# Mixing an attention output inside the attention's own tile shapes, in plain float32, with a new set of planner costs

## The chip, the cores and the metric

The kernel runs on 1 core of one Trainium2 chip. TensorE (PE) does the matmuls, and its weight loads are listed apart as PEld. VectorE (DVE), ScalarE (ACT), GpSimd (POOL) and SyncE (SP) each run their own instructions in the order in which they were written down; they wait for each other only through semaphores. The metric is the device time of the core in microseconds (us).

## The reference

```
scores = (1/sqrt(64)) * q @ k.T                  # 4 batches x 12 heads, 448 x 448
scores = cap * tanh(scores / cap)
attn   = softmax(scores)                         # rows of 448
x      = attn @ v, heads side by side            # 4 x 448 x 768
h      = x.T @ U @ V                             # U 448 x 32, V 32 x 448: mixes the 448 tokens
u      = x + h.T
out    = u + relu(u @ w_ch1) @ w_ch2             # 768 -> 3072 -> 768
```

## The kernel before, in words

The kernel keeps `u` transposed: for each batch one tile `u0` to `u3` of 128 partitions (two heads of 64) by 6 head pairs by 448 tokens. There are 24 head pairs in all.

The **attention stage** is written in groups of four head pairs (`four`). A score tile holds the two heads of a pair, each in 64 rows of the array (`scores`, line 459); ACT then does `tanh` on it (464), and one `exp` for two tiles (474). The products with `v` are lines 488 (the last 64 keys, 64x64 tiles) and 500 (128x64 tiles). DVE adds the exponentials up (506), and for every two pairs PE sums them over the partitions in 128x32 tiles (`sums`, 539 and 542). The sums are copied to `sr`, go through two small DMAs and a reciprocal on DVE, come back broadcast as `rb` (563), and DVE multiplies `u` by them (568).

The **mixing** (`mixin`, 12 times, each for two head pairs) is what is changed. Per mixing, PE turns `u` round in two steps of four transposes (590), ACT or DVE copies each result to `xx` as float32r (`high`), DVE subtracts that from the original to keep the lost low bits (`low`, 601), PE multiplies high and low parts with `ust`, which holds U in four blocks, the last of them U's own low bits (606, 4 matmuls of 256 columns in each step), the result `yp` is copied to `ys` and a low part of it made (617), and two matmuls with `vst` (626) give the two tiles `hh` that DVE adds to `u` (630). All these matmuls are float32r or transposes in the full 128x128 shape of the array; scores, products with `v` and sums are plain float32 in smaller tiles that run side by side.

The **second stage** (MoE in the code's names) is `u @ w_ch1`, relu and `@ w_ch2` in float32r matmuls of 448 columns (829, 894, 1021), on high and low parts, with Strassen-like savings. DVE and ACT make their operands. Some results are poured onto `u` by a DMA from a tile `st` (907).

The **order** on every engine is made when the kernel is built. Each piece is a task with a cost for each engine that may do it, a priority and its buffers; `simulate` runs the tasks through a list scheduler: when an engine is free it starts the ready task of the lowest priority number for which there are buffers. A task on PE whose `mode` differs from that of the task ahead is charged `SWITCH` (210) more. The tag `misc` has two PSUM banks, shared by sums, transposes, `yp` and `hh`. `fill` puts 18 dummy matmuls (385) into the first 25 us.

Of the kernel before, what the change touches and what calls it, by code (L numbers as in the profile page):

```python
# [11 lines left out]
F32 = mybir.dt.float32  # L12
F32R = mybir.dt.float32r
# [3 lines left out]
ALU = mybir.AluOpType  # L17

B, H, S, D = 4, 12, 448, 64
DM = H * D  # L20
FF = 4 * DM
R = 32
# [3 lines left out]
KT = 4  # L26
TM = S // KT
# [55 lines left out]

LAT = {"PE": 240, "ACT": 110, "DVE": 110, "POOL": 150, "SP": 0}
SWITCH = 210


class Plan:
# [43 lines left out]
    def simulate(self):  # L132
# [3 lines left out]
        mode = dict.fromkeys(LAT)  # L136
        head = dict.fromkeys(self.order, 0)
        locked = {"DVE": 0, "POOL": 0}
        events, out, now = [], [], 0
# [1 line left out]
            if not t.wait:  # L141
                heapq.heappush(events, (t.begin, 0, t.i, "r"))

        def room(b):
            if self.order[b.tag][head[b.tag]] is not b:
                return None
            for p in b.pools:
                if p.free[p.at(b)] and all(not q.due for q in p.after):
                    return p
            return None  # L150

        def can(t, e):
            if any(b.pool is None and not room(b) for b in t.bufs):
                return False
            if t.lock and e in locked and locked["POOL" if e == "DVE" else "DVE"] > now:
                return False
            if len(t.durs) > 1:
                for o, d in t.durs.items():
                    if o != e and d < t.durs[e]:
                        queue = sum(x.durs[o] for x in ready[o] if x is not t and (x.prio, x.i) < (t.prio, t.i))  # L160
                        if max(free[o] - now, 0) + queue + d <= t.durs[e]:
                            return False
            return True

        def start(t, e):
            for b in t.bufs:
                if b.pool is None:
                    p = room(b)
                    p.free[p.at(b)] -= 1
                    b.pool = p  # L170
                    b.slot = p.idle[p.at(b)].pop(0)
                    head[b.tag] += 1
            cost = t.durs[e] + (SWITCH if t.mode != mode[e] else 0)
            mode[e] = t.mode
            t.at, t.eng = now, e
            out.append(t)
            free[e] = now + cost
            if t.lock and e in locked:
                locked[e] = now + cost
            for o in t.durs:  # L180
                ready[o].remove(t)
            heapq.heappush(events, (now + cost, 1, t.i, "e"))
            heapq.heappush(events, (now + cost + (LAT[e] if t.lat is None else t.lat), 2, t.i, "d"))

        while True:
            for e in LAT:
# [7 lines left out]
            now = events[0][0]  # L194
            while events and events[0][0] == now:
                _, _, i, what = heapq.heappop(events)
                t = self.tasks[i]
# [63 lines left out]
class Build(Plan):  # L261
# [75 lines left out]
    def mixing_consts(self):  # L337
        nc = self.nc
        begin, prio = 15000, -150
        raw = self.buf("wr", [128, 2 * DM], I32, self.wq)  # L340
        raw2 = self.buf("wr", [128, 2 * DM], I32, self.wq)
        a, a2 = (self.buf("wa", [128, DM], F32, self.wp) for _ in range(2))
        n = KT * R
        ust = self.ust = self.buf("ust", [TM, KT, 4, R], F32R, self.aq)
        vst = self.vst = self.buf("vst", [128, S], F32R, self.aq)

        def load():
            nc.sync.dma_start(out=self.ident, in_=self.id_dram)
            nc.sync.dma_start(out=raw.t[:TM, :2 * n], in_=self.u.bitcast(I32))

        def load2():
            nc.sync.dma_start(out=raw2.t[:, :2 * S], in_=self.vv.bitcast(I32))

        def u_parts():
            ur = a.t[:TM, :n].rearrange("p (t r) -> p t r", t=KT)
            for i in range(3):
                nc.vector.tensor_copy(ust.t[:, :, i], ur)
            nc.vector.tensor_tensor(out=ust.t[:, :, 3], in0=ur, in1=ust.t[:, :, 0].bitcast(F32), op=ALU.subtract)

        def v_parts():  # L360
            vr = a2.t[:, :S]
            nc.vector.tensor_copy(vst.t, vr)
            nc.vector.tensor_tensor(
                out=vst.t[64:96], in0=vr[64:96], in1=vst.t[64:96].bitcast(F32), op=ALU.subtract)

        self.task({"SP": 700}, load, w=[(raw, "u"), (raw, "l"), ("ident", 0)], lat=4000, begin=begin, prio=prio)
        self.task({"SP": 400}, load2, w=[(raw2, "u"), (raw2, "l")], lat=4500, begin=begin, prio=prio)
        self.convert(raw, lambda: raw.t[:TM, :2 * n], a, lambda: a.t[:TM, :n], prio, n)
        self.task({"DVE": 800}, u_parts, r=[(a, 0)], w=[(ust, 0)], prio=prio)
        self.convert(raw2, lambda: raw2.t[:, :2 * S], a2, lambda: a2.t[:, :S], prio, S)  # L370
        self.task({"DVE": 900}, v_parts, r=[(a2, 0)], w=[(vst, 0)], prio=prio)


    def fill(self):
# [42 lines left out]
    def four(self, p):  # L417


        nc = self.nc  # L420
# [3 lines left out]
        for i in range(4):  # L424
            b, q = divmod(p + i, NP)
# [18 lines left out]
        for g in range(7):  # L444
# [3 lines left out]
            for j in range(2):  # L448
# [16 lines left out]

                r = [(qks[c], 0) for c in cs]
                if j == 0:
                    self.task({"PE": 750}, scores, r=r, w=[(ps, 0), (pss[1], "next")], prio=prio, mode="q" if t == 3 else "sc")
                else:
                    self.task({"PE": 750}, scores, r=[*r, (pss[1], "next")], w=[(ps, 0)], prio=-300, mode="q" if t == 3 else "sc")  # L470
                self.task({"ACT": 920}, tanh, r=[(ps, 0)], w=[(th, j)], prio=prio)
# [101 lines left out]
    def mixin(self, b, pp):  # L573

        nc = self.nc
        p = b * NP + 2 * pp + 1
        prio = p - 100
        u = self.u_bufs[b]
        yp = None
        ks = [(u, 2 * pp), (u, 2 * pp + 1)]  # L580
        for t0 in (0, 2):
            tp = self.psum("misc")
            yp = yp or self.psum("misc")
            xx = self.buf("xx", [TM, 2, 2, 256], F32R, self.aq)

            def transposes(t0=t0, tp=tp):
                for j in range(2):
                    for i in range(2):
                        tok = TM * (t0 + j)
                        nc.tensor.transpose(  # L590
                            tp.t[:TM, 256 * j + 128 * i:256 * j + 128 * i + 128], u.t[:, 2 * pp + i, tok:tok + TM],
                            self.ident)

            def view(tp):
                return tp.t[:TM].rearrange("p (t n) -> p t n", t=2)

            def high(e, tp=tp, xx=xx):
                self.copy(e, xx.t[:, 0], view(tp))

            def low(tp=tp, xx=xx):  # L600
                nc.vector.tensor_tensor(out=xx.t[:, 1], in0=view(tp), in1=xx.t[:, 0].bitcast(F32), op=ALU.subtract)

            def products(t0=t0, xx=xx):
                for i in range(2):
                    for j in range(2):
                        nc.tensor.matmul(
                            yp.t[:, :256], self.ust.t[:, t0 + j], xx.t[:, i, j], start=t0 + j + i == 0,
                            stop=t0 + j == KT - 1 and i == 1)

            self.task({"PE": 450}, transposes, r=[*ks, ("ident", 0)], w=[(tp, 0)], prio=prio, mode="mm")  # L610
            self.task({"ACT": 600, "DVE": 690}, high, r=[(tp, 0)], w=[(xx, 0)], prio=prio)
            self.task({"DVE": 690}, low, r=[(tp, 0), (xx, 0)], w=[(xx, 1)], prio=prio)
            self.task({"PE": 480}, products, r=[(xx, 0), (xx, 1), (self.ust, 0)], w=[(yp, 0)], prio=prio, mode="mm")
        ys = self.buf("ys", [128, 256], F32R, self.an)

        def y_low():
            nc.vector.tensor_tensor(
                out=ys.t[32:64], in0=yp.t[32:64, :256], in1=ys.t[32:64].bitcast(F32), op=ALU.subtract)

        self.task({"ACT": 380, "DVE": 400}, lambda e: self.copy(e, ys.t, yp.t[:, :256]), r=[(yp, 0)], w=[(ys, 0)], prio=prio)  # L620
        self.task({"DVE": 420}, y_low, r=[(yp, 0)], w=[(ys, 0)], prio=prio)
        for i in range(2):
            hh = self.psum("misc")

            def mix(i=i, hh=hh):
                nc.tensor.matmul(hh.t[:, :S], ys.t[:, 128 * i:128 * i + 128], self.vst.t, start=True, stop=True)

            def add(i=i, hh=hh):
                x = u.t[:, 2 * pp + i]
                nc.vector.tensor_tensor(out=x, in0=x, in1=hh.t[:, :S], op=ALU.add)  # L630

            self.task({"PE": 210}, mix, r=[(ys, 0), (self.vst, 0)], w=[(hh, 0)], prio=prio, mode="mm")
            self.task({"DVE": 620}, add, r=[(hh, 0)], w=[ks[i]], prio=prio)


# [472 lines left out]
```

## Time and profile before

| | |
|---|---|
| median of 3 runs | 866.02 us (864.76 to 869.65) |
| profiled execution, first to last instruction | 867.9 us |
| PE busy | 851.3 us (98%) |
| DVE busy | 678.5 us (78%) |
| ACT busy | 518.2 us (60%) |
| mean granted clock | 0.996 |

Of the profiled execution the span is the only time listed; it lies 1.9 us above the median and inside the range of the runs. Matmuls are pipelined, and PE counts as busy while one is under way, so 98% doesn't say that PE is at its peak: time that PE loses between two matmuls of different shapes is inside it. Where one group of matmuls starts and where the next one starts says more than the busy column.

### The profile page before, as it was taken

The numbers are of one execution on the slowest core, as the hardware profiler recorded it, in microseconds if no ns is written. First come the engines' busy times: TensorE is split into PE (matmuls) and PEld (weight loads), VectorE is DVE, ScalarE is ACT, GpSimd is POOL, SyncE is SP. The second block draws the span as 40 slices with busy tenths as digits, with TensorE's granted clock in tenths as the row PEclk, the third lists the DMA queues.
The fourth block names the chain that finished last, engine by engine and source line by source line (L and its number), as shares of the span: only waits on it lengthen the run. The fifth ranks groups of instructions, "written<-read, shape, count | busy, mean of one in ns | idle before, by whom it ended". The sixth has DMA issues, their size and how long they took to land.

```text
span 867.9 us, 11802 instructions
## 1 busy us (share of the span) xinstructions
PE 851.3 (98%) x4314; PEld 677.4 (78%) x4314; DVE 678.5 (78%) x1131; ACT 518.2 (60%) x771; POOL 134.2 (15%) x174
## 2 busy tenths in 40 slices
PE   9999998999999999998999999999999999999998
PEld 5343442435899999997999999999999999999997
DVE  2798887867987777876777789788888788888864
ACT  7999897987554555535554455455655555555610
POOL 0111111111121111211111111101111111211110
PEclk9999999999999999999999999999999999999999
DMA  6753344422578787897887754914426354452413
GB/s 220 251 166 102 119 140 133 129 65 60 147 212 263 207 248 204 221 244 215 220 249 203 231 161 92 269 40 98 133 43 163 77 137 96 78 164 42 98 33 128
DMA packets 49338, 132.38 MB, mean 153 GB/s; under 512 B 6496, under 2 KB 25344, under 8 KB 49280
## 3 DMA queue, kind: packets, MB, share of 16 engines
q1 hardware_dynamic: 23024, 79.29, 28.3%
q0 software_dynamic: 19344, 33.46, 21.3%
q10 hardware_dynamic: 6912, 18.88, 5.5%
q8 instruction: 34, 0.56, 0.3%
q14 instruction: 24, 0.20, 0.1%
HBM read 79.28 MB, written 24.47 MB: 120 GB/s over the span
## 4 chain that ended last, share of the span: by engine, by line
PE 53%; DVE 0%; issue 0%
PE mm L829 25%; PE mm L1021 15%; PE mm L894 13%; DVE cx L842 0%; DVE u L899 0%; DVE wa L308 0%
## 5 line engine op out<-in xcount | busy, mean ns | idle before, releaser
L829 PE MATMUL mm<-x,ws 128*128 128x448 f32 x1512 | 333.6, 367 | 1.2 <-DVE x L664 1.2
L829 PEld LDWEIGHTS mm<-x,ws 128*128 128x128 f32 x1512 | 283.7, 188 | 27.4 <-DVE x L664 1.5
L894 PE MATMUL mm<-g,w 128*128 128x448 f32 x864 | 188.1, 367 | 2.5 <-ACT st L254 2.0
L894 PEld LDWEIGHTS mm<-g,w 128*128 128x128 f32 x864 | 162.8, 189 | 17.3 <-ACT st L254 2.4
L1021 PE MATMUL mm<-g,w 128*128 128x448 f32 x630 | 139.9, 366 | 0.0
L254 ACT ACTIVATE st<-mm 128x448 f32<-128x448 f32 x121 | 65.9, 545 | 120.1 <-PE mm L894 61.8
L1021 PEld LDWEIGHTS mm<-g,w 128*128 128x128 f32 x630 | 118.2, 188 | 10.6
L907 POOL DMA_DIRECT2D u<-st x72 | 62.9, 873 | 265.1 <-ACT st L254 265.1
L464 ACT ACTIVATE th<-sc,qsc 128x896 f32<-128x896 f32 x84 | 80.5, 1005 | 11.2 <-PE sc L459 7.0
L899 DVE TENSOR_TENSOR u<-u,mm 128x448 f32<-128x448 f32 x96 | 59.4, 620 | 34.1 <-PE mm L894 32.3
L459 PE MATMUL sc<-qk 64*128 64x448 f32 (+1 forms) x384 | 76.8, 567 | 1.2 <-ACT th L464 1.2
L474 ACT ACTIVATE th<-th,capt 128x1792 f32<-128x1792 f32 x42 | 75.3, 1794 | 1.0
L1044 POOL DMA_DIRECT2D u<-st x45 | 38.8, 863 | 218.8 <-ACT st L254 173.8
L500 PE MATMUL o<-th,vn 128*64 128x448 f32 x288 | 59.4, 548 | 0.0
L664 DVE TENSOR_TENSOR ws<-ta,ws 128x384 fp32r<-128x384 f32 x96 | 52.9, 552 | 7.0 <-ACT ws L254 6.6
L308 DVE SCALAR_TENSOR_TENSOR wa<-wa,wr 128x768 int32<-128x768 int32 (+2 forms) x50 | 46.7, 936 | 14.1 <-ACT wa L300 13.2
L459 PEld LDWEIGHTS sc<-qk 64*128 64x128 f32 (+1 forms) x384 | 26.8, 173 | 34.4 <-issue 18.8
L506 DVE TENSOR_TENSOR es<-es,th 128x896 f32<-128x896 f32 (+1 forms) x36 | 39.1, 1087 | 11.6 <-ACT th L474 11.1
L300 ACT ACTIVATE wa<-wr 128x768 f32<-128x768 f32 (+2 forms) x50 | 44.0, 884 | 3.9 <-DMA kept<-wa 1.8
L254 ACT ACTIVATE cx<-mm 128x448 f32<-128x448 f32 x42 | 22.9, 545 | 38.0 <-PE mm L829 24.6
L500 PEld LDWEIGHTS o<-th,vn 128*64 128x64 f32 x288 | 18.5, 136 | 34.5 <-issue 32.4
L1039 DVE TENSOR_TENSOR u<-u,mm 128x448 f32<-128x448 f32 x45 | 27.9, 620 | 22.3 <-PE mm L1021 20.9
(116 smaller groups left out, 984.4 us busy)
## 6 DMA issues: line engine op xcount, KB each, us to landing
wr<-in_w SPq DMA_DIRECT2D x48, 768.0 KB, 5.8
u<-st POOLq DMA_DIRECT2D x117, 224.0 KB, 4.1
kept<-wa ACTq DMA_DIRECT2D x48, 384.0 KB, 5.9
qk<-in_qk SPq DMA_DIRECT2D x24, 448.0 KB, 4.1
wa<-kept SPq DMA_DIRECT2D x28, 384.0 KB, 4.0
wr<-kept SPq DMA_DIRECT2D x20, 384.0 KB, 4.0
vn<-in_v SPq DMA_DIRECT2D x12, 448.0 KB, 3.9
rb<-rd POOLq DMA_DIRECT2D x24, 224.0 KB, 3.9
```

Of the source, the lines that this page charges most:

```text
L254: e.activation(out=out, in_=in_, func=func)
L308: nc.vector.scalar_tensor_tensor(out=a_t().bitcast(I32), in0=a_t().bitcast(I32), scalar=3, in1=raw_t()[:, 0::2], op0=ALU.logical_shift_lef ...
L459: nc.tensor.matmul(ps.t[out, a, :S], qks[c].t[hd, 1, 128 * t:min(S, 128 * t + 128)], qks[c].t[hd, 0], start=True, stop=True)
L464: nc.scalar.activation(out=th.t[:, j], in_=ps.t[:, :, :S], func=AF.Tanh, scale=self.qsc)
L474: nc.scalar.activation(out=th.t, in_=th.t, func=AF.Exp, scale=self.capt)
L500: nc.tensor.matmul(o.t[64 * a:64 * a + 64, :S], vn.t[:, 3 * i + t, a], th.t[:, j, a], start=False, stop=t == 2)
L664: e.tensor_tensor(out=lo, in0=src(), in1=hi.bitcast(F32), op=ALU.subtract)
L829: nc.tensor.matmul(ps.t[:, :S], ws[p].t[:, wi, sl], xs[p].t[:, xi, d], start=fresh and n == 0, stop=n == 8, skip_group_check=not fresh)
L894: nc.tensor.matmul(ps.t[:, :S], w1[f].t[:, wi, sl], g[b, f].t[:, gi], start=f == fs[0] and i == 0, stop=f == fs[-1] and i == 2)
L899: nc.vector.tensor_tensor(out=u.t[:, d], in0=u.t[:, d], in1=ps.t[:, :S], op=ALU.add)
L907: nc.gpsimd.dma_start(out=u.t[:, d], in_=st.t, accum_op=ALU.add)
L1021: nc.tensor.matmul(ps.t[:, :S], w[:, wi, k, sl], g[gi][:, k], start=fresh and n == 0, stop=n == 5, skip_group_check=not fresh)
```

## The change

**The mixing.** One step of 16 transposes takes the place of two steps of four: each turns one head's 64 rows by 112 tokens, the two heads of a pair go into two `misc` banks, and their task has the mode `sc` of the score tiles. Two copies (ACT or DVE) put them into one float32 `xx`; no low parts are made. The products with U are 8 plain float32 matmuls of 128 columns into 32 partitions each (mode `s`, that of the sums), `ys` is 128 columns wide rather than 256, and the products with V are two plain float32 matmuls in 64 rows each (mode `sc`). `ust` holds U once, `vst` V, both float32.

**The planner.** ACT and DVE tasks occupy their engine for 75 and 60 less than their cost (`OVER`), and their results still come at the full cost. A task can now take several buffers of one tag at once (`rooms`). The first score tile of each two gets a priority lower by 3. As the order of all engines comes out of one simulation, it changes in the second stage too.

```diff
+OVER = {"ACT": 75, "DVE": 60}
...
-            cost = t.durs[e] + (SWITCH if t.mode != mode[e] else 0)
+            new = [b for b in t.bufs if b.pool is None]
+            for b, p in zip(new, rooms(new)):
...
+            cost = max(t.durs[e] - OVER.get(e, 0), 60) + (SWITCH if t.mode != mode[e] else 0)
...
-            heapq.heappush(events, (now + cost + (LAT[e] if t.lat is None else t.lat), 2, t.i, "d"))
+            heapq.heappush(events, (now + cost + OVER.get(e, 0) + (LAT[e] if t.lat is None else t.lat), 2, t.i, "d"))
...
-                    self.task({"PE": 750}, scores, r=r, w=[(ps, 0), (pss[1], "next")], prio=prio, mode="q" if t == 3 else "sc")
+                    self.task({"PE": 750}, scores, r=r, w=[(ps, 0), (pss[1], "next")], prio=prio - 3, mode="q" if t == 3 else "sc")
...
-            def low(tp=tp, xx=xx):
-                nc.vector.tensor_tensor(out=xx.t[:, 1], in0=view(tp), in1=xx.t[:, 0].bitcast(F32), op=ALU.subtract)
...
+        tps = [self.psum("misc") for _ in range(2)]
+        xx = self.buf("xx", [TM, KT, 2, 128], F32, self.aq)
+
+        def transposes():
+            for i in range(2):
+                for t in range(KT):
+                    for a in range(2):
+                        hd = slice(64 * a, 64 * a + 64)
+                        at = 64 * (2 * t + i)
                         nc.tensor.transpose(
+                            tps[a].t[:TM, at:at + 64], u.t[hd, 2 * pp + i, TM * t:TM * t + TM], self.ident[hd, hd])
+
+        self.task({"PE": 480}, transposes, r=[*ks, ("ident", 0)], w=[(tp, 0) for tp in tps], prio=prio, mode="sc")
+        for a, tp in enumerate(tps):
+            self.task({"ACT": 520, "DVE": 640}, lambda e, a=a, tp=tp: self.copy(
...
+        yp = self.psum("misc")
+
+        def products():
+            for h in range(2):
                 for i in range(2):
+                    for e in range(2):
+                        t = 2 * h + e
+                        rows = slice(32 * (2 * i + e), 32 * (2 * i + e) + 32)
                         nc.tensor.matmul(
+                            yp.t[rows, :128], self.ust.t[:, t, :R], xx.t[:, t, i], start=h == 0, stop=h == 1)
...
+        self.task({"PE": 450}, products, r=[(xx, 0), (xx, 1), (self.ust, 0)], w=[(yp, 0)], prio=prio, mode="s")
+        ys = self.buf("ys", [128, 128], F32, self.an)
...
+        hs = [self.psum("misc") for _ in range(2)]
+
+        def mix():
+            for i in range(2):
+                rows = slice(64 * i, 64 * i + 64)
+                nc.tensor.matmul(hs[i].t[:, :S], ys.t[rows], self.vst.t[rows], start=True, stop=True)
+
+        self.task({"PE": 760}, mix, r=[(ys, 0), (self.vst, 0)], w=[(hh, 0) for hh in hs], prio=prio, mode="sc")
```

What the order becomes is seen at three places. The first is PE's last mixing inside the attention stage, from a score tile to the last product with V. Before, `misc<-ident` (590) are the transposes, `misc<-xx,ust` (606) the products with U and `misc<-vst,ys` (626) those with V:

```order
L590 MATMUL misc<-ident,u_1382 112x128 x4
L459 MATMUL sc<-qk 128x448 x2
L459 MATMUL sc_1561<-qk 128x448 x2
L488 MATMUL o<-th,vn 64x448 x2
L488 MATMUL o_1574<-th,vn 64x448 x2
L606 MATMUL misc<-xx,ust 128x256 x4
L590 MATMUL misc<-ident,u_1382 112x128 x4
L459 MATMUL sc<-qk 128x448 x2
L459 MATMUL sc_1592<-qk 128x448 x2
L500 MATMUL o<-th,vn 64x448 x6
L606 MATMUL misc<-xx,ust 128x256 x4
L500 MATMUL o_1574<-th,vn 64x448 x6
```

After the change (lines 462 for 459, 491 for 488, 503 for 500, 542 and 545 for the sums, 592, 608 and 619 for the mixing):

```order
L462 MATMUL sc<-qk 128x448 x2
L462 MATMUL sc_1594<-qk 128x448 x2
L592 MATMUL misc<-ident,u_1409 112x64 x16
L491 MATMUL o<-th,vn 64x448 x2
L491 MATMUL o_1627<-th,vn 64x448 x2
L503 MATMUL o<-th,vn 64x448 x6
L608 MATMUL misc<-xx,ust 32x128 x8
L503 MATMUL o_1627<-th,vn 64x448 x6
L619 MATMUL misc<-vst,ys 128x448 x2
```

Four groups of the 128x128 shape between other shapes have become three groups, and the transposes stand right behind score tiles, whose shape they share.

The second place is PE at the end of the attention stage, where the first second-stage products (`mm<-x,ws`) come in between. Before:

```order
L829 MATMUL mm<-x,ws 128x448 x9
L606 MATMUL misc<-xx,ust 128x256 x4
L829 MATMUL mm<-x,ws 128x448 x9
L590 MATMUL misc<-ident,u_1382 112x128 x4
L829 MATMUL mm<-x,ws 128x448 x18
L606 MATMUL misc<-xx,ust 128x256 x4
L829 MATMUL mm<-x,ws 128x448 x18
L626 MATMUL misc<-vst,ys 128x448 x2
```

After (824 for 829):

```order
L824 MATMUL mm<-x,ws 128x448 x9
L592 MATMUL misc<-ident,u_1409 112x64 x16
L824 MATMUL mm<-x,ws 128x448 x9
L608 MATMUL misc<-xx,ust 32x128 x8
L824 MATMUL mm<-x,ws 128x448 x9
L619 MATMUL misc<-vst,ys 128x448 x2
L824 MATMUL mm<-x,ws 128x448 x27
```

Here the mixing stood between matmuls of its own shape before, and now stands between matmuls of another one.

The third place is ACT in one mixing of the attention stage, where `th<-sc` is tanh, `th<-th` exp, and `sr`, `xx` are copies from PSUM. Before:

```order
L464 ACTIVATE th<-sc_618,qsc 128x896
L254 ACTIVATE sr<-misc 128x448
L254 ACTIVATE xx<-misc 112x512
L474 ACTIVATE th<-th,capt 128x1792
L464 ACTIVATE th<-sc,qsc 128x896
L254 ACTIVATE xx<-misc 112x512
L464 ACTIVATE th<-sc_649,qsc 128x896
```

After (467 for 464, 477 for 474, 263 for 254):

```order
L467 ACTIVATE th<-sc_624,qsc 128x896
L263 ACTIVATE sr<-misc 128x448
L477 ACTIVATE th<-th,capt 128x1792
L467 ACTIVATE th<-sc,qsc 128x896
L263 ACTIVATE xx<-misc 112x8x64 x2
L467 ACTIVATE th<-sc_651,qsc 128x896
```

Both copies to `xx` now stand together, an exp behind the copy of the sums and ahead of the second tanh.

## Rows read from the trace of the kernel before

**Rows 1.** Busy time in three stretches (us, instructions in brackets), granted clock, DMA.

```profile
45.00:205.00 160.00, 156.03 (x890) 62.16 (x890) 127.54 (x188) 140.17 (x142) 22.82 (x39) 0.99 0.39 118
205.00:240.00 35.00, 31.68 (x171) 26.25 (x170) 31.66 (x58) 20.27 (x39) 3.28 (x5) 1.00 0.42 121
240.00:868.00 628.00, 622.12 (x3037) 570.74 (x3035) 495.45 (x848) 318.54 (x553) 104.25 (x120) 1.00 0.60 157
```

**Rows 2.** PE's timeline around one mixing: start, length, engine, line, tiles, shapes, matmuls.

```profile
188.88 0.67 PE L626 MATMUL misc<-vst,ys 128*128 128x448 f32 x2
189.48 2.48 PE L500 MATMUL o<-th,vn 128*64 128x448 f32 x12
...
193.53 0.65 PE L590 MATMUL misc<-ident,u 128*112 128x128 f32 x4
194.11 1.77 PE L459 MATMUL sc<-qk 64*128 64x448 f32 x8
195.81 0.98 PE L488 MATMUL o<-th,vn 64*64 64x448 f32 x8
196.72 0.74 PE L606 MATMUL misc<-xx,ust 112*128 112x256 f32 x4
197.31 0.60 PE L590 MATMUL misc<-ident,u 128*112 128x128 f32 x4
197.84 1.77 PE L459 MATMUL sc<-qk 64*128 64x448 f32 x8
199.54 2.48 PE L500 MATMUL o<-th,vn 128*64 128x448 f32 x12
201.94 0.74 PE L606 MATMUL misc<-xx,ust 112*128 112x256 f32 x4
202.61 2.48 PE L500 MATMUL o<-th,vn 128*64 128x448 f32 x12
```

**Rows 3.** Who PE waited for, whole span: us in total, times, longest.

```profile
PE misc L539 <- DVE es L506: 2.7, 1, 2.7
...
PE mm L894 <- ACT st L254: 2.0, 1, 2.0
```

**Rows 4.** Busy time in two stretches of 25 us with a lower clock.

```profile
125.00:150.00 25.00, 22.32 (x120) 8.09 (x114) 19.23 (x32) 20.08 (x20) 2.39 (x5) 0.93 0.48 140
400.00:425.00 25.00, 22.70 (x104) 20.18 (x103) 16.68 (x29) 11.45 (x21) 3.65 (x5) 0.93 0.78 233
```

**Rows 5.** The waits of DVE from 133 to 146 us, and of ACT from 380 to 412.

```profile
DVE u L568 <- DMA rb<-rd: 4.4, 1, 4.4
...
ACT cx L254 <- DMA u<-st: 4.8, 1, 4.8
ACT st L254 <- DMA u<-st: 3.3, 1, 3.3
```

**Rows 6.** The DMAs that write `rb`, all of them.

```profile
DMA to landing us min/median/max: 3.3/3.9/8.8
```

**Rows 7.** The waits of ACT from 45 to 205 us.

```profile
ACT th L464 <- PE sc L459: 6.6, 12, 1.0
ACT x L254 <- DVE wr L657: 3.9, 1, 3.9
```

**Rows 8.** Groups of the mixing by shape: busy us, mean ns of one, idle before.

```profile
L601 DVE TENSOR_TENSOR xx<-misc,xx 112x512 fp32r<-112x512 f32 x24 | 16.5, 686 | 2.0 <-ACT xx L254 1.5
L254 ACT ACTIVATE xx<-misc 112x512 fp32r<-112x512 f32 x16 | 9.6, 599 | 3.2 <-PE misc L590 3.1
L617 DVE TENSOR_TENSOR ys<-misc,ys 32x256 fp32r<-32x256 f32 x12 | 5.0, 418 | 0.6 <-ACT ys L254 0.2
```

**Rows 9.** Two tanh back to back on ACT (timeline), and tanh and exp as groups.

```profile
198.91 1.91 ACT L464 ACTIVATE th<-sc,qsc 128x896 f32<-128x896 f32 x2
...
L464 ACT ACTIVATE th<-sc,qsc 128x896 f32<-128x896 f32 x84 | 80.5, 1005 | 11.2 <-PE sc L459 7.0
L474 ACT ACTIVATE th<-th,capt 128x1792 f32<-128x1792 f32 x42 | 75.3, 1794 | 1.0
```

More of the change, by code (lines that the diff above doesn't have):

```diff
@@ L142, in simulate, with rooms @@
                 heapq.heappush(events, (t.begin, 0, t.i, "r"))
[L144 to L150, printed above, removed]
+        def rooms(bufs):
+            taken, n, out = {}, {}, []
+            for b in bufs:
+                k = n.get(b.tag, 0)
+                if self.order[b.tag][head[b.tag] + k] is not b:
+                    return None
+                n[b.tag] = k + 1
+                for p in b.pools:
+                    at = p, p.at(b)
+                    if p.free[at[1]] > taken.get(at, 0) and all(not q.due for q in p.after):
+                        taken[at] = taken.get(at, 0) + 1
+                        out.append(p)
+                        break
+                else:
+                    return None
+            return out
         def can(t, e):
-            if any(b.pool is None and not room(b) for b in t.bufs):
+            if rooms([b for b in t.bufs if b.pool is None]) is None:
                 return False
@@ L165, in start @@
         def start(t, e):
[L166 to L172, printed above, removed]
-            cost = t.durs[e] + (SWITCH if t.mode != mode[e] else 0)
+            new = [b for b in t.bufs if b.pool is None]
+            for b, p in zip(new, rooms(new)):
+                p.free[p.at(b)] -= 1
+                b.pool = p
+                b.slot = p.idle[p.at(b)].pop(0)
+                head[b.tag] += 1
+            cost = max(t.durs[e] - OVER.get(e, 0), 60) + (SWITCH if t.mode != mode[e] else 0)
             mode[e] = t.mode
@@ L343, in mixing_consts @@
         n = KT * R
-        ust = self.ust = self.buf("ust", [TM, KT, 4, R], F32R, self.aq)
-        vst = self.vst = self.buf("vst", [128, S], F32R, self.aq)
+        ust = self.ust = self.buf("ust", [TM, KT, 4 * R], F32, self.aq)
+        vst = self.vst = self.buf("vst", [128, S], F32, self.aq)
         def load():
@@ L352, in load2, with keep_u, keep_v @@
             nc.sync.dma_start(out=raw2.t[:, :2 * S], in_=self.vv.bitcast(I32))
[L354 to L364, printed above, removed]
+        def keep_u():
+            nc.vector.tensor_copy(ust.t[:, :, :R], a.t[:TM, :n].rearrange("p (t r) -> p t r", t=KT))
+        def keep_v():
+            nc.vector.tensor_copy(vst.t, a2.t[:, :S])
         self.task({"SP": 700}, load, w=[(raw, "u"), (raw, "l"), ("ident", 0)], lat=4000, begin=begin, prio=prio)
@@ L368, in mixing_consts @@
         self.convert(raw, lambda: raw.t[:TM, :2 * n], a, lambda: a.t[:TM, :n], prio, n)
-        self.task({"DVE": 800}, u_parts, r=[(a, 0)], w=[(ust, 0)], prio=prio)
+        self.task({"DVE": 200}, keep_u, r=[(a, 0)], w=[(ust, 0)], prio=prio)
         self.convert(raw2, lambda: raw2.t[:, :2 * S], a2, lambda: a2.t[:, :S], prio, S)
-        self.task({"DVE": 900}, v_parts, r=[(a2, 0)], w=[(vst, 0)], prio=prio)
+        self.task({"DVE": 400}, keep_v, r=[(a2, 0)], w=[(vst, 0)], prio=prio)
     def fill(self):
@@ L578, in mixin @@
         u = self.u_bufs[b]
-        yp = None
         ks = [(u, 2 * pp), (u, 2 * pp + 1)]
[L581 to L589, printed above, removed]
-                        nc.tensor.transpose(
[L591 to L598, printed above, removed]
-            def low(tp=tp, xx=xx):
-                nc.vector.tensor_tensor(out=xx.t[:, 1], in0=view(tp), in1=xx.t[:, 0].bitcast(F32), op=ALU.subtract)
-            def products(t0=t0, xx=xx):
+        tps = [self.psum("misc") for _ in range(2)]
@@ L604, in products @@
+        for a, tp in enumerate(tps):
+            self.task({"ACT": 520, "DVE": 640}, lambda e, a=a, tp=tp: self.copy(
+                e, xx.t.rearrange("p t i n -> p (t i) n")[:, :, 64 * a:64 * a + 64],
+                tp.t[:TM].rearrange("p (m n) -> p m n", n=64)), r=[(tp, 0)], w=[(xx, a)], prio=prio)
+        yp = self.psum("misc")
+        def products():
+            for h in range(2):
                 for i in range(2):
-                    for j in range(2):
+                    for e in range(2):
+                        t = 2 * h + e
+                        rows = slice(32 * (2 * i + e), 32 * (2 * i + e) + 32)
@@ L606, in products @@
                         nc.tensor.matmul(
[L607 to L626, printed above, removed]
+                            yp.t[rows, :128], self.ust.t[:, t, :R], xx.t[:, t, i], start=h == 0, stop=h == 1)
@@ new lines, in mixin @@
+        self.task({"PE": 450}, products, r=[(xx, 0), (xx, 1), (self.ust, 0)], w=[(yp, 0)], prio=prio, mode="s")
+        ys = self.buf("ys", [128, 128], F32, self.an)
+        self.task({"ACT": 240, "DVE": 250}, lambda e: self.copy(e, ys.t, yp.t[:, :128]), r=[(yp, 0)], w=[(ys, 0)], prio=prio)
+        hs = [self.psum("misc") for _ in range(2)]
[3 more added lines that the diff above has]
+                nc.tensor.matmul(hs[i].t[:, :S], ys.t[rows], self.vst.t[rows], start=True, stop=True)
@@ L628, in add @@
+        self.task({"PE": 760}, mix, r=[(ys, 0), (self.vst, 0)], w=[(hh, 0) for hh in hs], prio=prio, mode="sc")
+        for i, hh in enumerate(hs):
             def add(i=i, hh=hh):
@@ L630, in add @@
                 nc.vector.tensor_tensor(out=x, in0=x, in1=hh.t[:, :S], op=ALU.add)
-            self.task({"PE": 210}, mix, r=[(ys, 0), (self.vst, 0)], w=[(hh, 0)], prio=prio, mode="mm")
             self.task({"DVE": 620}, add, r=[(hh, 0)], w=[ks[i]], prio=prio)
```

## The prediction

> **What bounds the kernel now.** I read the busy table by stretches first [rows 1]. From 240 us on PE runs float32r matmuls and nothing else: 3037 in 622.12 us, 0.205 us each, without a gap but for one. DVE (495 of 628 us) and ACT (319) have room. The change leaves the number of these matmuls as it is, so that stage is a fixed block unless a wait in it comes or goes. From 45 to 205 us, the attention, PE is busy 156.0 of 160 us, ACT 140.2 (88%) and DVE 127.5 (80%). PE is the first limit there and ACT is near behind it. From 205 to 240 us second-stage products begin between the last mixings; PE idles 3.3 us.
>
> Next I read PE's timeline in the attention from start to start [rows 2], since its lengths overlap. Groups follow each other without a wait: PE sets the pace. A plain float32 matmul of 448 columns goes through in rounds, all tiles of a shape side by side: a 64x64 group (488, two rounds) holds PE from 195.81 to 196.72, 0.91 us; two score tiles (four rounds) 1.70; the six products of line 500 (six rounds) 2.40. The straight line through these is 0.373 us for a round and 0.165 us for each group. I take 0.165 as the price of a change of shape.
>
> Last the waits. PE waited 2.7 us at one sum (539) and 2.0 us at one product of the second stage (894) [rows 3]. After each the granted clock in 25 us is 0.93 [rows 4]: some of the stretch was at the lower level (1.2 of 2.4 GHz), a loss of 0.07 x 25 = 1.7 us each. The first came from DVE, which stood 4.4 us in front of the normalizing multiply for `rb`, the second from ACT, which stood 3.3 us for a buffer that a pouring DMA still read [rows 5]. `rb` lands in 3.9 us as a rule and in 8.8 at worst [rows 6]. So two late DMAs cost 2.7 + 1.7 = 4.4 and 2.0 + 1.7 = 3.7 us, 8.1 together.
>
> **The change part by part.**
>
> *Mixing on PE, removed.* From start to start [rows 2]: transposes 0.58 (193.53 to 194.11), products and transposes together 1.12 (196.72 to 197.84), products 0.67, product with V 0.60: 2.97 us in four groups. Without the price of four changes (0.66) it is 2.31.
>
> *Added.* Transposes: four of 128 columns take 0.58 - 0.165 = 0.42, 0.105 each; 64 columns are half of that, 0.053, and if the two halves of the array work side by side as two score tiles do, 16 take 8 x 0.053 = 0.42. They stand behind score tiles in the same shape and cost no change. If neither held, 16 x 0.105 = 1.68 is the upper bound; 0.42 is the lower one. I take 0.45, because they differ from score matmuls, which do run side by side, in columns alone. Products with U: four tiles side by side, two steps of two rounds of 128 columns, 4 x 0.373 x 128/448 = 0.43. With V: two halves side by side, one matmul of two rounds, 0.75, beside score tiles mostly. The sum is 1.63 against 2.31, 0.68 less. As the same four products took 0.59 and 0.67 in two places, the price of a change may be underestimated for them, so I take 0.6.
>
> The objection is that plain float32 is slow. By the rows a round pair costs 2 x 0.373 = 0.75 us against 0.205 for a float32r matmul of the same columns, 3.6 times as much. The Trainium skill ("FP8 and Floating Point Precision", TensorE Precision Notes) says that true FP32 takes 4 passes through the array. By that the product with V would be 4 x 0.205 = 0.82, 0.07 more per mixing, 0.8 us in all; the trace agrees to that degree, and what pays for the passes is that two or four tiles run at once and that no low parts are multiplied.
>
> *Changes of shape on PE*, counted in the two orders: 143 before the first second-stage product, now 112; behind it 2, now 15. Ten mixings lie ahead of that point in both. Attention: 10 x 0.6 + 31 x 0.165 = 6.0 + 5.1 = 11.1 us less on PE. Transition: 13 x 0.165 - 2 x 0.6 = 0.9 us more.
>
> *DVE and ACT.* DVE loses 24 x 0.69 and 12 x 0.42 us of low parts, 21.6 us [rows 8]; the copies to `xx` stay 24 of the same size. That is time on an engine that isn't the limit: nothing directly, but DVE is then less often late for PE. ACT loses little: up to the last exp its order has 2 more copies to `xx` (0.6 each), 2 fewer of `sr`, 3 fewer of `u`, 2 fewer of small operands, and half-width `ys`, about 2.5 us less. If the attention got all of the 11.1 us, ACT would be busy 137.7 of 148.9 us, 92%. It waits today 6.6 us for scores, twelve times, and 3.9 us once behind DVE [rows 7]; the score waits should shrink, with PE faster and the first score tiles ahead of other work. I give 2 of the 11.1 us back to new waits for ACT: 9.
>
> *New waits.* The 16 transposes need both `misc` banks, so they wait for the copy of the sums just ahead. Behind them in PE's order stand the products with `v`, and on ACT the second tanh waits behind both copies to `xx`. In between are two score tiles, 1.70 us, and a copy takes 0.6: hidden, unless the copy comes behind an exp (1.8 us [rows 9]), when PE would lose about 1 us there. This is within the 2 us.
>
> *Planner costs.* Two tanh of 1.005 us take 1.91 together [rows 9], so tails do overlap on the chip, by 0.1; the planner's 0.075 is inside that. No instruction gets faster by it; the order fits the chip better, which I cost at nothing in the second stage: PE has no idle to lose there but for late DMAs. Those depend on what else is moving, and the order of all loads changes. I count half of their 8.1 us as gone, 4.0. U and V prepared in two copies rather than six small DVE instructions ends before the first mixing: nothing.
>
> *Sum*, against the profiled span: 867.9 - 9.0 + 0.9 - 4.0 = 855.8. This execution lay 1.9 us above the median of the runs, so the median after is 855.8 - 1.9 = 853.9. I give 854.
>
> **The rivals.**
>
> *All of it comes*: the whole 11.1 in the attention, nothing lost in the transition (PE waits there anyway), both late DMAs gone: 867.9 - 11.1 - 8.1 - 1.9 = 846.8. For it: ACT's score waits; against it: new loads, new coincidences.
>
> *ACT takes over*: the attention shortens only by what ACT loses, 2.5 us, and the late DMAs remain: 867.9 - 2.5 + 0.9 - 1.9 = 864.4. For it: 88% busy and strictly in order. Against it: 19.8 us of ACT idle in that stretch [rows 1], most of it waits for PE or behind DVE.
>
> *The transposes don't scale* (slower): each of the 16 brings its own weights, 112 columns as before; if loads and not columns set the 0.105 us, and the halves don't overlap, they take 1.68 us, 1.23 more per mixing, 14.8 us in 12. 854 + 14.8 = 868.8. It decides from about 0.08 us per transpose, where (0.08 x 16 - 0.45) x 12 = 10 us eat the gain of PE. For it: columns and weights are 128 and 112, so the 0.105 can't tell them apart; against it: scores in pairs. On the page the Trainium skill ("TensorE: Matmul & The Clock Gate", LDWEIGHTS) gives columns / 1.2 in ns, whatever the rows; by this estimate 112 columns are 93 ns, and eight pairs 0.75 us, which would make it 3.6 us slower than my sum, 857.5. No row of before separates the two.
>
> *New late DMAs*: the reordered second stage meets three more waits of 4 us: 854 + 12 = 866. Only one showed there in 628 us.
>
> **How the numbers follow.** My forecast has a chance of 0.58, all of it 0.17, ACT 0.13, the transposes 0.06, new waits 0.06. The likeliest alone runs from 850 to 859. The range: below, all of it, 846.8, and a little for what DVE's relief may add: 846; above, ACT's case, 864. That leaves out the two last and some edge, under 2 in 10. A difference of under 0.5% (4.3 us) is about what a measurement of this kernel can't tell from none: faster means below 861.7. That is nearly all of the forecast, all of the second and a third of ACT's case: 0.78. Same: most of ACT's case and parts of the last two, 0.15. Slower 0.07.
>
> **What the profile after would show.** Start to start, 16 transposes at 0.45 us behind score tiles without a gap (near 1.7 would be the slow rival); products with U at 0.43 + 0.165, those with V at 0.75 beside scores. The first second-stage product starts some 9 us earlier, or 13 if the late `rb` doesn't come back. ACT over 90% busy in the attention and its score waits shorter; DVE some 20 us less busy. From 240 us on (less the shift) 0.205 us per matmul. I'm wrong if ACT's waits are replaced by PE waiting for tanh in the same sum, or if new gaps stand in the second stage.

## The result and the profile after

The changed kernel takes 854.34 us (median of 4 runs, 849.83 to 856.12), the kernel before 866.82 in the same comparison (4 runs, 864.76 to 869.65). The ratio is 0.9831, with a 95% interval from 0.9800 to 0.9861: faster by 1.4 to 2.0%.

The profiled execution after is the fastest of the four: its time is 849.83, its span 847.9. So the two profiles lie 20.0 us apart and the medians 12.5, and what follows from the profiles has to be read with that. The busy table by stretches, with the same columns as [rows 1]:

```profile
45.00:194.00 149.00, 147.44 (x1095) 57.21 (x1091) 113.77 (x168) 139.71 (x146) 22.81 (x39) 1.00 0.41 122
194.00:229.00 35.00, 30.97 (x190) 25.64 (x191) 28.36 (x51) 16.92 (x32) 4.91 (x7) 0.95 0.57 169
229.00:848.00 619.00, 615.31 (x3015) 565.39 (x3013) 494.23 (x850) 312.61 (x540) 101.82 (x119) 1.00 0.59 157
```

In the attention PE is now busy 147.4 of 149 us and ACT 139.7, 94% against 88% before. The second stage runs at 615.31 / 3015 = 0.204 us per matmul, as before. PE's timeline around one mixing, as in [rows 2], and the first product of the second stage:

```profile
117.28 1.77 PE L462 MATMUL sc<-qk 64*128 64x448 f32 x8
118.89 0.62 PE L592 MATMUL misc<-ident,u 64*112 64x64 f32 x16
119.43 0.98 PE L491 MATMUL o<-th,vn 64*64 64x448 f32 x8
120.35 2.48 PE L503 MATMUL o<-th,vn 128*64 128x448 f32 x12
122.75 0.65 PE L608 MATMUL misc<-xx,ust 112*32 112x128 f32 x16
123.33 1.77 PE L462 MATMUL sc<-qk 64*128 64x448 f32 x8
124.93 0.96 PE L619 MATMUL misc<-vst,ys 64*128 64x448 f32 x4
...
187.79 2.09 PE L824 MATMUL mm<-x,ws 128*128 128x448 f32 x9
```

From start to start, transposes take 0.54 us (118.89 to 119.43), products with U 0.58, and the score tiles ahead of the transposes 1.61 rather than 1.70: no change of shape follows them now. The same first product stood here before:

```profile
205.73 2.12 PE L829 MATMUL mm<-x,ws 128*128 128x448 f32 x9
```

It has come forward by 17.9 us. PE's waits over the whole span are different ones from [rows 3]:

```profile
PE misc L592 <- ACT sr L263: 2.8, 1, 2.8
PE misc L592 <- issue: 1.9, 1, 1.9
...
PE misc L592 <- DVE u L571: 1.2, 1, 1.2
```

The sum that waited 2.7 us for DVE is gone, and the 2.0 us in the second stage too. The 1.9 us that the page puts down to "issue" are the first transposes of all. They read what DVE's multiply by `rb` writes, and that multiply, which had itself stood for the broadcast, ended just ahead of them, at 42.06 + 1.09 = 43.15 us. DVE's and PE's timelines there:

```profile
42.06 1.09 DVE L571 TENSOR_TENSOR u<-u,rb 128x896 f32<-128x896 f32 x1 [1.97 <-DMA rb<-rd]
...
43.25 0.66 PE L592 MATMUL misc<-ident,u 64*112 64x64 f32 x16 [1.89 <-issue]
```

New is a wait of 2.8 us at the transposes of a later mixing (592) for the copy of the sums. ACT's timeline shows why:

```profile
191.75 1.50 ACT L263 ACTIVATE x<-wr 128x448 fp32r<-128x448 f32 x3
193.15 2.89 ACT L263 ACTIVATE x<-u 128x448 fp32r<-128x448 f32 x6
195.95 0.52 ACT L263 ACTIVATE sr<-misc 128x448 f32<-128x448 f32 x1
```

The copy stands behind nine operand copies. It holds one of the two `misc` banks, and the transposes now need both. In the busy table of the 25 us around, the mean granted clock is 0.93, so part of the stretch was at the lower level, as behind the two waits of [rows 4]:

```profile
175.00:200.00 25.00, 22.21 (x159) 11.72 (x158) 16.82 (x28) 16.74 (x25) 3.07 (x5) 0.93 0.19 52
```

### The profile page after: what moved, and what is told of

Same layout as the page of the kernel before. It is cut to its first block, busy times and chain, and to the rows that moved or that the text cites. A ratio compares the mean times of both kernels' runs of the same rounds, so it can differ in the third digit from the quotient of the medians.

```text
span 847.9 us, 12162 instructions
## 1 busy us (share of the span) xinstructions
PE 835.2 (99%) x4530; PEld 666.6 (79%) x4530; DVE 660.9 (78%) x1106; ACT 508.5 (60%) x756; POOL 133.6 (16%) x174
## 4 chain that ended last, share of the span: by engine, by line
PE 93%; DVE 2%; ACT 2%; DMA 2%; issue 1%; POOL 0%; ACTq 0%; DVEq 0%; POOLq 0%
PE mm L824 35%; PE mm L889 24%; PE mm L1016 15%; PE sc L462 7%; PE o L503 6%; PE o L491 1%; ACT th L467 1%; PE misc L388 1%; PE misc L542 1%; PE misc L619 1%; DMA rd<-r 1%; PE misc L608 1%; ACT th L477 1%; DVE x L659 1%; DMA r<-sr 1%
## 5 line engine op out<-in xcount | busy, mean ns | idle before, releaser
L1016 PE MATMUL mm<-g,w 128*128 128x448 f32 x630 | 139.7, 366 | 0.0
L894 DVE TENSOR_TENSOR u<-u,mm 128x448 f32<-128x448 f32 x96 | 59.2, 618 | 20.0 <-PE mm L889 18.4
L263 ACT ACTIVATE ws<-wa 128x384 fp32r<-128x384 f32 x48 | 24.5, 521 | 38.3 <-PE mm L824 38.3
```

What stands on the lines that cost most here:

```text
L263: e.activation(out=out, in_=in_, func=func)
L894: nc.vector.tensor_tensor(out=u.t[:, d], in0=u.t[:, d], in1=ps.t[:, :S], op=ALU.add)
L1016: nc.tensor.matmul(ps.t[:, :S], w[:, wi, k, sl], g[gi][:, k], start=fresh and n == 0, stop=n == 5, skip_group_check=not fresh)
```

## The experiments

All medians below come from 5 or more runs. The kernel before had 869.07, 869.03 and 868.62 us in the three sessions. They lie within 0.5 us of each other, so medians of different sessions are set against each other too. The ratios are taken inside a session. "The three places" are the first score tile's priority, lower by 3.

**The parts alone.** The mixing with the planner's old settings:

```diff
-OVER = {"ACT": 75, "DVE": 60}
+OVER = {}
...
-                    self.task({"PE": 750}, scores, r=r, w=[(ps, 0), (pss[1], "next")], prio=prio - 3, mode="q" if t == 3 else "sc")
+                    self.task({"PE": 750}, scores, r=r, w=[(ps, 0), (pss[1], "next")], prio=prio, mode="q" if t == 3 else "sc")
```

> The new mixing with the planner's old costs (no shortened ACT and DVE tasks) and the first score tiles at their old place. My theory: the gain is PE time taken out of the attention stage by the mixing (fewer rounds, fewer changes of shape), so this gets most of it: 7 to 11 us below the kernel before, with the first second-stage product 9 to 14 us earlier. Rival: the planner's costs make the gain (ACT packed more tightly), and this gets 0 to 4 us.

The new settings with the old `mixin` and `mixing_consts`:

> The old float32r mixing with the planner's new costs and the first score tiles three places ahead. My theory: 0 to 3 us below the kernel before, since PE's work in the attention stage is unchanged and PE was busy there 156 of 160 us. Rival: 6 us or more below it.

Mixing and new costs without the three places, so the second edit above alone:

> The changed kernel with the first score tiles back at their old priority. My theory: within 2 us of the changed kernel, 852 to 857, as ACT's waits for scores were 6.6 us in the attention stage before. Rival: these waits come back whole (7 us instead of 2.6), and it takes 858 or more.

Mixing and three places without the new costs, so the first edit alone:

> The new mixing with the first score tiles three places ahead, but the planner's old costs. With the mixing alone at 867.1 and mixing with new costs at 864.6 us, the changed kernel at 854.7, the three places seem to carry 10 us. Theory: they give PE a regular order (sums, two score tiles, transposes, products, in the same rhythm for every two pairs), and the mixing's shorter PE time then comes through: 853 to 858 without the new costs too. Rival: only both together give it, 862 or more.

And the changed kernel again:

> The changed kernel once more, for a second profile. Its runs lay between 849.8 and 856.1, and the profiled one was the fastest. Expected: a median of 853 to 855, and a profile that shows in the slower execution one or two waits for a DMA that landed late, 3 to 4 us each, which the first profile doesn't have. Rival: the executions differ in many small waits, or in the length of the attention stage.

| kernel | median us | ratio to before (95%) |
|---|---|---|
| old mixing, new settings | 870.9 | 1.0004 (0.9985 to 1.0023) |
| new mixing, old settings | 867.1 | 0.9969 (0.9951 to 0.9986) |
| new mixing, new costs | 864.6 | 0.9954 (0.9928 to 0.9981) |
| new mixing, three places | 860.8 | 0.9904 (0.9871 to 0.9937) |
| all (the changed kernel) | 854.7 | 0.9822 (0.9797 to 0.9846) |

My theory said that the mixing alone would bring 7 to 11 us. It brings 2. The rival on record for it has the number right, 0 to 4, and the reason wrong: the settings alone bring nothing that can be measured. The new costs add 2.5 us to the mixing and the three places 6.3 (867.1 to 860.8), and together they add 12.4. The run with the three places and the old costs lies between the two ranges on record for it, 853 to 858 and 862 or more.

The run without the three places was expected within 2 us of the changed kernel and came out 10 us above. By its number the rival on record came true: ACT's waits for scores, from 45 to 200 us, are back, and the time is above 858.

```profile
ACT th L467 <- PE sc L462: 7.0, 11, 2.0
```

So that run alone doesn't tell ACT's waits from those of DVE that follow.

Where the mixing's time went is seen in the kernel with the mixing alone: first the busy table of one stretch.

```profile
45.00:187.00 142.00, 133.63 (x962) 49.60 (x964) 107.53 (x158) 120.72 (x123) 20.59 (x35) 0.96 0.43 131
```

What PE waited for there from 45 to 204 us:

```profile
PE misc L592 <- DVE u L571: 5.0, 2, 3.6
PE misc L542 <- DVE es L509: 3.4, 2, 2.4
```

And DVE's waits for the broadcast from 45 to 235 us:

```profile
DVE u L571 <- DMA rb<-rd: 16.2, 6, 3.7
```

The same stretch of the changed kernel's busy table:

```profile
45.00:187.00 142.00, 140.71 (x1058) 53.31 (x1056) 108.57 (x157) 135.58 (x139) 22.81 (x39) 1.00 0.42 126
```

And its waits of DVE for the broadcast, again to 235 us:

```profile
DVE u L571 <- DMA rb<-rd: 5.5, 3, 3.2
```

With the mixing alone PE idles 8.4 of 142 us, against 1.3, and the clock is 0.96 of full, some 5 us more. Its first second-stage product comes at 204.41 us, 16.6 later than in the changed kernel. DVE stands at the normalizing multiply, and PE waits for it in two ways. The transposes read what the multiply writes. At the first mixing this cost most, 3.6 us and then a clock of 0.75 from 40 to 50 us and 0.91 from 50 to 60, another 3.4 us. DVE's and PE's timelines there:

```profile
44.86 1.09 DVE L571 TENSOR_TENSOR u<-u,rb 128x896 f32<-128x896 f32 x1 [3.28 <-DMA rb<-rd]
...
46.01 1.10 PE L592 MATMUL misc<-ident,u 64*112 64x64 f32 x16 [3.62 <-DVE u L571]
```

And behind the multiply in DVE's order stand additions that PE's sums need. DVE's timeline, later:

```profile
141.34 1.09 DVE L571 TENSOR_TENSOR u<-u,rb 128x896 f32<-128x896 f32 x1 [3.73 <-DMA rb<-rd]
142.35 1.08 DVE L509 TENSOR_TENSOR es<-es,th 128x896 f32<-128x896 f32 x1
```

PE's timeline there:

```profile
143.49 0.58 PE L542 MATMUL misc<-es,ones 128*32 128x448 f32 x3 [2.42 <-DVE es L509]
```

DVE waits 3.7 us, the addition comes late, and PE waits 2.4 us for it. This is the stall that the kernel before had once [rows 5]. Without the three places DVE's waits are as long:

```profile
DVE u L571 <- DMA rb<-rd: 16.6, 6, 4.5
```

The second profile of the changed kernel (span 854.6, 6.7 us more than the first) shows what made these two executions differ. The wait of the second stage is back, and ahead of it ACT stood for a buffer that a pouring DMA still read:

```profile
PE mm L889 <- ACT st L263: 2.0, 1, 2.0
...
ACT st L263 <- DMA u<-st: 4.4, 1, 4.4
```

The busy table has the lower clock behind it:

```profile
275.00:300.00 25.00, 23.03 (x106) 20.81 (x106) 16.67 (x30) 9.72 (x17) 4.28 (x5) 0.93 0.71 195
```

That is 3.7 of the 6.7 us, as the expectation had it; the attention stage is longer by 2.5 (first product at 190.29), which is the rival's part. Most of this is the clock again: the first transposes waited 2.2 us here, and the granted clock from 40 to 50 us is 0.83, 1.7 us lost, where it is 1.00 in the first profile.

**Slack for the broadcast.** If DVE's standing at the multiply is the loss, it can be kept from standing there by telling the planner that the broadcast lands later, so that other work is written down ahead of the multiply:

```diff
-        self.task({"POOL": 1100}, get, r=[("rd", p)], w=[(rb, 0)], lat=3400, prio=prio)
+        self.task({"POOL": 1100}, get, r=[("rd", p)], w=[(rb, 0)], lat=6900, prio=prio)
```

Without the three places:

> The changed kernel without the three places, but the planner is told that the broadcast of the reciprocals lands 3.5 us later (6900 rather than 3400), so that DVE's multiply by it stands later in DVE's order. Without the three places DVE stood 16.6 us for these DMAs in six waits, against 5.5 in three with them. Theory A: these waits are the loss, and slack gives it back: 853 to 859. Theory B: the loss is PE's irregular order itself (ten score tiles in a row that wait for tanh, transposes right behind the multiply), and it stays at 862 to 868 though DVE waits less.

Measured: 855.9, 0.9857 (0.9825 to 0.9889), against 864.6. DVE's waits for the broadcast fell to this:

```profile
DVE u L571 <- DMA rb<-rd: 2.7, 1, 2.7
```

On the mixing alone:

> The new mixing alone (old costs, old places; 867.1 us), with the later broadcast in the plan. Theory A: the mixing's PE time was there all along and was lost to DVE standing at its multiplies; 856 to 861. Theory B: without the new costs or places the order stays bad for other reasons; 863 or more.

Measured: 860.6, 0.9903 (0.9876 to 0.9930), against 867.1: inside theory A's range, at its upper end. DVE's waits for the broadcast fell from 16.2 us to 4.1, while ACT's waits for scores stayed nearly what they were, 9.5 us before and 7.7 now (45 to 200 us):

```profile
DVE u L571 <- DMA rb<-rd: 4.1, 3, 2.4
...
ACT th L467 <- PE sc L462: 7.7, 9, 4.4
```

On the kernel before:

> The kernel before with the later broadcast in the plan, nothing else. Its DVE stood 5.7 us in three waits for the broadcast, and PE lost 4.4 us behind one of them. Theory: 2 to 5 us below the kernel before; if it gains as much as it gave the kernel without the three places (8.7 us), slack is a gain of its own and says nothing about the mixing.

Measured: 875.1, 1.0074 (1.0053 to 1.0096): slower, where I expected 2 to 5 us less. On the changed kernel:

> The changed kernel, with the three places, and the planner told that the broadcast lands 3.5 us later. Theory A (standing DVE multiplies are what the three places avoid): little is left to avoid here, DVE waits 5.5 us in all, so 851 to 855, at most 3 us below the changed kernel. If it is slower than 856, the slack costs buffers and only helps where the order is bad.

Measured: 859.1, 0.9905 (0.9877 to 0.9932), 4.4 us slower than the changed kernel and above theory A's range.

So slack is no gain of its own. It gives back 8.7 and 6.5 us where DVE stood 16 us at the multiply, and costs 4 to 6 where it stood under 6 (and 9 in one more kernel, at the end of this section). In the kernel before with slack, PE waits at the old products 5.3 us, where it had waited 0.4 without:

```profile
PE misc L606 <- DVE xx L601: 5.3, 3, 2.5
```

There the mixing comes later (its first transposes start at 46.12 rather than 43.38 us), and PE reaches its next step before DVE has made the low parts. DVE's standing at the multiply is thus the likeliest reason for the larger part of what the mixing lost: slack gives back 8.7 of the 9.9 us lost without the three places and 6.5 of the 12.4 lost by the mixing alone. It is not shown alone, as slack moves other tasks with the multiply. Without the three places ACT's waits for scores fell too, from 7.0 us to 4.0. Nor is it shown that the three places work by DVE's waits alone: with slack and three places DVE waits only 1.2 us for the broadcast, and the kernel is slower than with the three places alone.

**The transposes.** All of one half of the array's rows first:

```diff
-            for i in range(2):
-                for t in range(KT):
-                    for a in range(2):
+            for a in range(2):
+                for i in range(2):
+                    for t in range(KT):
```

> The changed kernel with the 16 transposes in another order: all eight of one head of the pairs (one half of the array's rows), then all eight of the other, so that neighbours can't run side by side. If columns set their pace, 16 x 0.053 = 0.85 us rather than 0.45 per mixing, 5 us in 12, and 857 to 860 in all; if the weight loads overlap anyway and pairs gain nothing, 854 to 856.

Measured: 857.3, 0.9863 (0.9833 to 0.9893), some 2.6 us more than the changed kernel, though the two intervals overlap. PE's timeline at one mixing:

```profile
60.77 0.89 PE L592 MATMUL misc<-ident,u 64*112 64x64 f32 x16
61.58 2.48 PE L503 MATMUL o<-th,vn 128*64 128x448 f32 x12
```

The step takes 0.81 us instead of 0.54, both with the change of shape that follows: 0.27 more, 3.2 in twelve mixings. Neighbours in different halves do overlap. The loss is under the 5 us expected because the unpaired step is shorter than I had set it. Against score tiles alone (1.70 in [rows 2]) the pairs add 1.61 + 0.54 - 1.70 = 0.45, just as in the sum, and the unpaired ones 1.61 + 0.81 - 1.70 = 0.72, not 0.85.

**The copy of the sums first.** An attempt to take away the new wait:

```diff
-        self.task({"DVE": 620, "ACT": 560}, lambda e: self.copy(e, sr.t, s.t[:, :S]), r=[(s, 0)], w=[(sr, 0)], prio=prio)
+        self.task({"DVE": 620, "ACT": 560}, lambda e: self.copy(e, sr.t, s.t[:, :S]), r=[(s, 0)], w=[(sr, 0)], prio=prio - 10)
```

> The changed kernel with the copy of the sums ten places ahead. In the changed kernel the last but one mixing's transposes waited 2.8 us for that copy, which stood behind nine operand copies on ACT, and the clock fell behind the wait (3.4 us at half). Theory: this wait and the clock's loss go, 2 to 5 us: 850 to 853. Rival: products and the rest of the mixing now follow the transposes at once and PE waits for their copies instead: within 1 us of the changed kernel.

Measured: 850.3 (846.4 to 851.8), 0.9777 (0.9744 to 0.9810), at the lower end of the theory's range: the fastest kernel here, some 4.5 us under the changed kernel, though the two intervals overlap a little. PE's timeline at the place:

```profile
195.02 0.66 PE L592 MATMUL misc<-ident,u 64*112 64x64 f32 x16
196.72 0.64 PE L608 MATMUL misc<-xx,ust 112*32 112x128 f32 x16 [1.04 <-ACT xx L263]
198.26 1.02 PE L619 MATMUL misc<-vst,ys 64*128 64x448 f32 x4 [0.89 <-ACT ys L263]
```

Its busy table of the same 25 us as above:

```profile
175.00:200.00 25.00, 23.07 (x184) 10.87 (x181) 16.50 (x28) 18.31 (x27) 3.07 (x5) 1.00 0.17 41
```

The transposes start at once. In place of one wait of 2.8 us stand two of about 1 us, as the rival said, but no lower clock follows them: that saves 1.7 us more. From the first second-stage product on, this profile is some 3 us shorter than the first one of the changed kernel (657.0 against 660.1), and ahead of it 1.6 longer (189.34 against 187.79). Where the rest of the 4.5 us between the medians comes from is not shown. With slack as well:

> The changed kernel with both additions: the copy of the sums ten places ahead (850.3 alone) and the later broadcast in the plan. If they act on different waits, 846 to 850; if the slack adds nothing, 849 to 852.

Measured: 859.7, 0.9900 (0.9874 to 0.9925), above both ranges and 9.4 us more than the earlier copy alone. The slack's cost stays, and the gain of the earlier copy isn't seen beside it: the transposes wait 2.1 us for the multiply in the same place, and the clock from 200 to 210 us is 0.66, another 3.4 us lost.

```profile
201.37 0.76 PE L592 MATMUL misc<-ident,u 64*112 64x64 f32 x16 [2.08 <-DVE u L571]
```

## Why the time was right, and where the reasons were not

The median met the forecast, 854.34 against 854, more closely than the terms met theirs. Against the profile before, in the first and the second profile after:

| term, us | sum | first | second |
|---|---|---|---|
| up to the first second-stage product, without the late broadcast | -9.0 | -13.5 | -11.0 |
| from there on, without the late DMA | +0.9 | +1.6 | +2.1 |
| the two late DMAs | -4.0 | -8.1 | -4.4 |
| all | -12.1 | -20.0 | -13.3 |

Errors of the terms cancel in part, and the execution that one takes moves the sum by 6.7 us. That the median is hit to within 0.4 us is luck.

*The mixing on PE* went nearly as priced. The three groups take 0.54 + 0.58 + 0.90 = 2.02 us in the rows above, against 2.97 in [rows 2], and the score tiles ahead take 0.09 less, not the 0.165 at which a change of shape was priced: 1.04 in this mixing. Added up in PE's timelines over the ten mixings ahead of the second stage, from start to start and without waits, its groups take 19.8 us rather than 30.8 and the score tiles 72.1 rather than 74.1: 13.0 less, where the sum had 11.1. The slow rival for the transposes is out: 16 of them in 0.54 us, with the change of shape. By the Trainium skill ("TensorE: Matmul & The Clock Gate", LDWEIGHTS) a load of 112 columns is 93 ns by estimate, so that eight pairs would take 0.75 us. The 0.54 us of the trace don't bear that out.

*The attention* got more than the 9.0 of the sum: 17.9 in the profiled execution, of which 4.4 are the late broadcast of before (2.7 and the clock's 1.7), and 15.4 in the second profile. The 2 us that I gave back to ACT were not lost: ACT went to 94% busy, and its waits for scores, from 45 to 194 us, fell from 6.6 us [rows 7] to 2.6:

```profile
ACT th L467 <- PE sc L462: 2.6, 6, 0.7
```

*The transition* cost more than 0.9, by the table 1.6 and 2.1. The new wait for `misc` was foreseen, at "about 1 us" and only behind an exp. It came behind nine operand copies and took 2.8 us, in the first profile with 1.7 of clock.

*The planner's settings* are the step that failed: "the order fits the chip better, which I cost at nothing in the second stage". For the attention, where they decide, the sum has no term for them at all; it takes PE's shorter mixing, less 2 us for ACT, for the gain. With the old settings, the mixing's 10 us and more come back as waits and lower clock, but for 2. I had taken the number of shape changes from the changed order, and looked at that order for waits only around the transposes. The mixing alone has 111 changes of shape ahead of the second stage, where the changed kernel has 112, so the count could not tell the two apart. What I should have priced, as far as the runs with slack show, is how much room there is between each DMA chain's end and the in-order instruction that waits for it. The rival "ACT takes over" gave a gain of 1.6 us, close to the 2 of the mixing alone, but ACT's load doesn't make it: ACT is busy 120.7 of 142 us there, 85%, less than in the changed kernel.

*The late DMAs*, half of 8.1 us: the first is gone in both profiles, the second in one of them. So 4.4 to 8.1 us went, where the sum had 4.0. The half was a guess and not read from the order.

Still open is by which of its effects the earlier score tile keeps PE's rhythm, and why slack costs a good order 4 to 9 us; both would take a kernel in which only the multiply's place on DVE is moved.

## What to carry to other kernels

When one table of costs and priorities sets the order of five engines, time taken off the busiest engine isn't had until the order is right again: here a mixing that is 10 us shorter on PE gave 2 us under the old settings and 14 under new ones that brought nothing measurable alone. Look in the new order for instructions that wait for a DMA on an in-order engine, and at what stands behind them. A wait of some 2 us on PE often cost nearly double here, as the clock's 1.7 us came on top; two waits of 1 us in the kernel with the earlier copy did not.

## What was not expected of the hardware

In six profiles (before, after twice, the mixing alone, the unpaired transposes, the sums first) PE waited 15 times for 1.9 us or longer behind its first 5 us, and 10 of these waits were followed by a stretch at the lower clock, some 1.7 us lost each, and 3.4 behind the first of the mixing alone. Waits of equal length were followed by it in one execution and not in another: the 2.8 us at the transposes cost it in the first profile of the changed kernel and not in the second. Shorter waits close together were followed by it too. In the kernel before with slack, PE waited three times for 0.8 to 0.9 us between 240 and 245 us:

```profile
240.00:250.00 10.00, 7.44 (x23) 5.84 (x22) 6.56 (x11) 3.57 (x6) 0.00 (x0) 0.66 0.77 250
```

The clock, and a DMA that landed late in one execution alone, make up most of the 6.7 us between the two profiles of the changed kernel; for the other executions it is not shown.
